# Column tiles of 32 instead of 64 for the packed up tail in a fused attention and gated feed-forward kernel

## The chip, the cores and the metric

One core of a Trainium2 chip runs the whole kernel. The metric is the device time of one execution in microseconds (us). The kernel before takes 195.24 us, the median of three runs (195.07 to 195.54). The profiler's span is some 1.7 us shorter, 193.5 us for the profiled execution, and the granted clock of TensorE in it was 1.000.

## The reference

One residual block over 2048 tokens of width 512, all in bfloat16. A layer norm feeds two branches, and both are added to the input.

```python
def reference(...):                                    # cut
    xn = layernorm(A_x)
    # A: 32 heads of 16; each token attends to itself and 7 earlier ones, 2 apart
    qkv = xn @ A_wqkv
    logits[h, s, w] = q[h, s] . k[h, s - 2 w] * 16 ** -0.5      # masked for s < 2 w
    o = softmax(logits) @ v[h, s - 2 w]
    a = o @ A_wo
    # B: gated feed-forward, inner width 1376 = 10 * 128 + 96
    b = (gelu(xn @ B_w_gate) * (xn @ B_w_up)) @ B_w_down
    return A_x + a + b
```

## The kernel before

The kernel is a list of tasks, one per group of instructions of one engine, with the buffers that they read and write. A list scheduler orders them by priority and puts in the semaphores; the table `SHIFT` moves groups of tasks up and down in priority. The 2048 tokens go through in four blocks of 512.

The inner width of 1376 leaves a tail of 96 columns after ten full tiles of 128. The gate tail, with 32 of the up columns, is one ordinary group of four 512-column matmuls (L1409). The other 64 up columns are packed: the 512 tokens are cut into two halves of 256, and each half goes into its own 64 columns of the array, so that two matmuls run side by side. They share one task with the sums over head elements that make the attention logits, which use four 32-column tiles side by side. I call this task the logit group.

```python
def mk_r(...):                     # the logit group of one block, on TensorE (L1208, L1215)
    def f(e):
        for kt in range(4):
            for c in range(2):     # two tiles of 64 columns, 256 tokens each
                ins = e.matmul(PS[64 * c:64 * c + 64, 512 * itu.slot:512 * itu.slot + 256],
                               lhsT=Wt[:, kt, 128:192],
                               rhs=xnT[:, itx.slot, kt, 256 * c:256 * c + 256],
                               start=(kt == 0), stop=(kt == 3), tile_position=(0, 64 * c))
        for (g, prs) in grp:       # 4 x 2 rounds of four tiles of 32 columns, 512 elements each
            for wq in range(2):
                for sj in range(4):
                    ins = e.matmul(PS[32 * sj:32 * sj + 32, ...], lhsT=E8[:, 24 - 8 * g:56 - 8 * g],
                                   rhs=UNI[:, prs[wq].slot, :, sj * 128:(sj + 1) * 128],
                                   start=(g == 0), stop=(g == 3), tile_position=(0, 32 * sj))
        return ins
```

The weighted sum over values (L1342) is also made of rounds of four 32-column tiles, and in blocks 1 and 2 it directly precedes the logit group. The other lines named below are the query, key and value projections (L1077 in block 0's start, L1131 elsewhere), the feed-forward matmuls (L1374), and the final accumulation over the attention output and the down projection (L1449, L1453).

Of the kernel before, what the change touches and what calls it, by code (L numbers as in the profile page):

```python
# [145 lines left out]
class Graph:  # L146
# [478 lines left out]


SHIFT = {
    "acc0": 223, "acc1": 3251, "er1": 857, "er2": 1563, "er3": -682, "ffn0": 185, "ffn1": -481, "ffn3": 9,
    "fin1": -264, "fin2": 595, "fin3": -2, "h0": -264, "h1": 24, "h2": 384, "h3": 81, "ldb0": 811,
    "ldb2": 200, "ldb3": -487, "ln1": 29, "ln2": 123, "ln3": -821, "prod0": 131, "prod1": -198, "pv0": 31,  # L630
    "pv1": -32, "pv2": 2520, "pv3": -241, "pvr0": 93, "pvr1": 556, "pvr2": 1268, "qkv1": 36, "qkv3": 44,
    "sm0": 114, "sm1": 276, "sm2": 146,
}
SCHED = dict(PE_SLACK=1.6, DMA_BPUS=250e3,
             TOL=dict(pe=0.3, act=-0.3, dve=0.3, pool=-0.3, sp=0.0))
# [24 lines left out]
def d_dve(n, rate=1.04):  # L660
    return 0.07 + n * rate * 1e-3
# [6 lines left out]
def bass_parallel_sum__sliding_local_dilated__glu_gated_geglu__prompt_kernel(nc, A_x, A_wqkv, A_wo, B_x, B_w_gate, B_w_up, B_w_down, out, dbg=None, cfg=None):  # L668
# [41 lines left out]
    with contextlib.ExitStack() as es:  # L710
        block = es.enter_context(nc.Block())

        def sb(name, shape, dt):
            return es.enter_context(nc.sbuf_tensor(name, shape, dt))
# [4 lines left out]
        Wt = sb("Wt", [128, 4, 192], BF)  # L719
        Wd = sb("Wd", [128, NJ, 512], BF)  # L720
        Wo = sb("Wo", [128, 4, 512], BF)
        xnT = sb("xnT", [128, NXT, 4, 512], BF)
# [32 lines left out]
        PS = es.enter_context(nc.psum_tensor("PS", [128, 4096], F32))  # L755
# [302 lines left out]
        for b in range(NB):  # L1058
# [119 lines left out]
            for g in range(4):  # L1178
                prs = []
                for wq in range(2):  # L1180
                    it_pr = pr_items[g][wq]
                    prs.append(it_pr)

                    def mk_p(wq=wq, g=g, it=it_pr, itq=it_qt, itk=KTI[b]):
                        return lambda e: e.tensor_tensor(  # L1185
                            out=UNI[:, it.slot, :, :],
                            in0=bass.AP(QT, (itq.slot * 4 + g) * 512, [[NQT * 4 * 512, 128], [0, 4], [1, 512]]),
                            in1=bass.AP(KT, (itk.slot * 4 + g) * 528 + 4 - 2 * wq, [[2 * 4 * 528, 128], [4, 4], [1, 512]]),
                            op=ALU.mult)
                    rdk = ([(KTI[0], ("t", t)) for t in range(4)] if b == 0 else [(KTI[b], g)]) + [(KTI[b], "pad")]  # L1190
                    rdq = [(it_qt, ("t", t)) for t in range(4)] if b == 0 else [(it_qt, (g, 0))]
                    t_of["pr%d_%d_%d" % (b, wq, g)] = G.task("dve", "pr%d_%d_%d" % (b, wq, g), d_dve(2048, 0.52), mk_p(),
                           rd=rdq + rdk, wr=[(it_pr, "d")] + ([(q, "a") for gg in range(g, g + ER_MERGE) for q in pr_items[gg]
                                                      if q is not it_pr] if g % ER_MERGE == 0 and wq == 0 else []),
                           prio=base + 20)

                er_grp.append((g, prs))
                if len(er_grp) < ER_MERGE:
                    continue

                it_u10 = Item("u%d_10" % b, P_ps, "ffn")

                def mk_r(grp=list(er_grp), lg=it_lg, itu=it_u10, itx=XTI[b]):
                    def f(e):
                        ins = None
                        for kt in range(4):
                            for c in range(2):
                                ins = e.matmul(PS[64 * c:64 * c + 64, 512 * itu.slot:512 * itu.slot + 256],  # L1208
                                               lhsT=Wt[:, kt, 128:192],
                                               rhs=xnT[:, itx.slot, kt, 256 * c:256 * c + 256],  # L1210
                                               start=(kt == 0), stop=(kt == 3), tile_position=(0, 64 * c))
                        for (g, prs) in grp:
                            for wq in range(2):
                                for sj in range(4):
                                    ins = e.matmul(  # L1215
                                        PS[32 * sj:32 * sj + 32, 512 * (lg.slot + wq):512 * (lg.slot + wq) + 512],
                                        lhsT=E8[:, 24 - 8 * g:56 - 8 * g],
# [3 lines that stand above are left out]
                    return f  # L1221
                G.task("pe", "er%d_%d" % (b, g), 0.4315 * (ER_MERGE + 1), mk_r(),
                       rd=[q for g_ in er_grp for q in g_[1]] + [I_E8, XTI[b], (I_wt, 2)],
                       wr=[it_lg, it_u10], prio=base + 5, mode="c", util=0.8)
                er_grp = []
# [316 lines left out]
```

## Time and profile before

| | kernel before |
|---|---|
| time, median of 3 | 195.24 us |
| span of the profiled execution | 193.5 us |
| busy: TensorE, VectorE, ScalarE | 97%, 79%, 54% |
| chain that ended last: TensorE | 93% |
| TensorE's waits for other engines after 6.3 us | none |
| last accumulation group begins; last addition begins | 190.22 us; 191.10 us |

The page's chain is followed back from the last instruction, and the views of waits name what an engine waited for. The prediction below shows the lines that carry this. The end of the kernel before, from the timeline (start us, us, engine, line, form; the bracket gives the idle time before it and what ended it):

```profile
190.22 0.78 PE L1453 MATMUL PS<-Wd,HT 128*128 128x128 bf16 x11
191.10 0.29 DVE L1473 TENSOR_TENSOR OB<-PS,XR 128x128 bf16<-128x128 f32 x1 [0.55 <-PE PS L1453]
```

The last addition begins 0.88 us after the last group of matmuls begins, and what it waits for is TensorE.

### The profile page before, as it was taken

Reading aid. Unit: us, or ns where it says so; the run is one execution under the profiler, and the core shown is the slowest. Engines: PE = TensorE matmul, PEld = TensorE weight load, DVE = VectorE, ACT = ScalarE, POOL = GpSimd, SP = SyncE. Lnnn points to the kernel's source line nnn. Section 1 sums busy time; section 2 is a strip of 40 time slices with the busy share of each in tenths; the row PEclk is TensorE's granted clock in tenths of the full one; section 3 lists DMA queues with packets and bytes.
Section 4 is the critical chain, followed back from the end, with each engine's and each line's share of the span. In section 5 each row is a group of like instructions: output and inputs, shape, how many; then the busy total and the mean of one; then the engine's idle time right before and its main releaser. Section 6 shows DMA issues by size and latency. Waiting matters only on the chain.

```text
span 193.5 us, 3221 instructions
## 1 busy us (share of the span) xinstructions
PE 187.4 (97%) x1207; PEld 91.6 (47%) x1224; DVE 153.2 (79%) x241; ACT 104.0 (54%) x171; POOL 16.2 (8%) x31
## 2 busy tenths in 40 slices
PE   6899999999999999999999999999999999999994
PEld 2794444444444444444444444444444444444484
DVE  5898999999998988995895699988997089931132
ACT  3587583996676665501667777328266640048000
POOL 6013001014711000000200000000000000000000
DMA  5999999898375006953511587420250298130121
GB/s 134 354 396 305 327 168 178 216 277 186 71 181 106 2 3 160 234 156 105 181 36 50 140 216 157 130 77 0 68 128 21 62 243 189 54 112 0 44 79 41
DMA packets 34800, 27.03 MB, mean 140 GB/s; under 512 B 11265, under 2 KB 33249, under 8 KB 34785
## 3 DMA queue, kind: packets, MB, share of 16 engines
q1 hardware_dynamic: 34784, 26.83, 54.6%
q8 instruction: 9, 0.15, 0.3%
q14 instruction: 7, 0.05, 0.1%
HBM read 19.99 MB, written 5.26 MB: 131 GB/s over the span
## 4 chain that ended last, share of the span: by engine, by line
PE 93%; ACT 2%; DVE 2%; DMA 1%; issue 1%; DVEq 0%
PE PS L1374 34%; PE PS L1453 20%; PE PS L1131 18%; PE PS L1449 7%; PE PS L1077 4%; PE PS L1342 4%; PE PS L1215 4%; PE PS L1409 1%; PE PS L1208 1%; DMA XIN<-in_A_x_dram 1%; ACT OT L1354 1%; DVE st L937 1%; PE PS L1019 0%; ACT UU L1391 0%; DVE XIN L976 0%
## 5 line engine op out<-in xcount | busy, mean ns | idle before, releaser
L1453 PE MATMUL PS<-Wd,HT 128*128 128x512 bf16 (+2 forms) x207 | 41.2, 345 | 0.1
L1374 PE MATMUL PS<-xnT,Wu 128*128 128x512 bf16 x157 | 39.9, 379 | 0.3 <-issue 0.2
L1374 PE MATMUL PS<-xnT,Wg 128*128 128x512 bf16 x154 | 39.3, 379 | 0.7 <-issue 0.5
L1185 DVE TENSOR_TENSOR UNI<-QT,KT 128x2048 bf16<-128x2048 bf16 x32 | 37.2, 1221 | 2.3 <-PE PS L1342 1.5
L1384 ACT ACTIVATE GG<-PS 128x512 bf16<-128x512 f32 x40 | 23.8, 601 | 26.5 <-PE PS L1374 23.1
L1131 PE MATMUL PS<-xnT,Wqkv 128*128 128x512 bf16 x156 | 34.8, 379 | 0.3 <-issue 0.2
L1391 ACT ACTIVATE UU<-PS 128x512 bf16<-128x512 f32 x40 | 24.0, 599 | 15.6 <-PE PS L1374 15.6
L1396 DVE TENSOR_TENSOR HT<-GG,UU 128x512 bf16<-128x512 bf16 x40 | 16.2, 418 | 17.3 <-ACT UU L1391 17.1
L1453 PEld LDWEIGHTS PS<-Wd,HT 128*128 128x128 bf16 x209 | 19.6, 98 | 18.6
L1374 PEld LDWEIGHTS PS<-xnT,Wg 128*128 128x128 bf16 x160 | 15.4, 98 | 19.4 <-issue 0.8
L1374 PEld LDWEIGHTS PS<-xnT,Wu 128*128 128x128 bf16 x160 | 15.5, 98 | 19.3 <-issue 0.8
L1131 PEld LDWEIGHTS PS<-xnT,Wqkv 128*128 128x128 bf16 x160 | 15.5, 98 | 18.8 <-ACT OT L1354 0.4
L1473 DVE TENSOR_TENSOR OB<-PS,XR 128x512 bf16<-128x512 f32 (+2 forms) x19 | 11.4, 602 | 11.8 <-PE PS L1453 11.6
L1322 DVE TENSOR_TENSOR UNI<-BS,PT 128x2048 bf16<-128x2048 bf16 x16 | 19.5, 1219 | 0.6 <-DMA PT<-pt_scratch 0.5
L1322 DVE TENSOR_TENSOR BS<-BS,PT 128x2048 bf16<-128x2048 bf16 x16 | 19.6, 1222 | 0.3
L1449 PE MATMUL PS<-Wo,OT 128*128 128x512 bf16 (+2 forms) x75 | 16.7, 345 | 0.1
L1148 ACT ACTIVATE KT<-PS 128x512 bf16<-128x512 f32 x12 | 7.3, 606 | 14.3 <-PE PS L1131 14.3
L1155 ACT ACTIVATE VT<-PS 128x512 bf16<-128x512 f32 x16 | 9.6, 597 | 4.4 <-PE PS L1131 4.4
L937 DVE BATCH_NORM_STATS2 st<-XIN 128x6 f32<-128x512 bf16 x16 | 10.7, 685 | 1.0 <-DMA XIN<-in_A_x_dram 1.0
L1171 POOL COPY KT<-KT 128x64 bf16<-128x64 bf16 x3 | 7.6, 2518 | 40.0 <-ACT KT L1148 38.6
L1354 ACT ACTIVATE OT<-PS 128x512 bf16<-128x512 f32 x16 | 8.3, 602 | 4.3 <-PE PS L1342 4.3
L1449 PEld LDWEIGHTS PS<-Wo,OT 128*128 128x128 bf16 x76 | 7.2, 98 | 7.0
(66 smaller groups left out, 150.3 us busy)
## 6 DMA issues: line engine op xcount, KB each, us to landing
BS<-vt_scratch SPq DMA_DIRECT2D x64, 128.5 KB, 3.5
vt_scratch<-VT SPq DMA_DIRECT2D x16, 128.0 KB
XR<-in_A_x_dram SPq DMA_DIRECT2D x16, 128.0 KB, 2.2
out_dram<-OB SPq DMA_DIRECT2D x14, 128.0 KB, 2.1
Wqkv<-in_A_wqkv_dram SPq DMA_DIRECT2D x3, 512.0 KB
XIN<-in_A_x_dram SPq DMA_DIRECT2D x6, 256.0 KB, 5.8
Wg<-in_B_w_gate_dram SPq DMA_DIRECT2D x1, 1280.0 KB
Wu<-in_B_w_up_dram SPq DMA_DIRECT2D x1, 1280.0 KB
```

Source lines behind the costliest of these rows:

```text
L937: return lambda e: e.bn_stats(out=st[:, t, :], in_=XIN[:, it.slot, t2, :])
L1131: ins = e.matmul(PS[:, 512 * it.slot:512 * it.slot + HWD], lhsT=lhsT, rhs=xnT[:, itx.slot, kt, c0:c0 + HWD], start=(kt == 0), stop=(kt == 3))
L1185: return lambda e: e.tensor_tensor(out=UNI[:, it.slot, :, :], in0=bass.AP(QT, (itq.slot * 4 + g) * 512, [[NQT * 4 * 512, 128], [0, 4], [1, ...
L1322: return lambda e: e.tensor_tensor(out=dst(), in0=bass.AP(BS, it.slot * 4 * 514 + o, [[NBS * 4 * 514, 128], [514, 4], [128, 4], [1, 128]]) ...
L1354: return lambda e: e.activation(out=OT[:, ito.slot, dq, :], in_=PS[:, 512 * it.slot:512 * it.slot + 512], func=ACTF.Identity)
L1374: ins = e.matmul(PS[0:M, 512 * it.slot:512 * it.slot + 512], lhsT=Wx[:, kt, j * 128:j * 128 + M], rhs=xnT[:, itx.slot, kt, :], start=(kt = ...
L1384: return lambda e: e.activation(out=GG[0:M, ito.slot, :], in_=PS[0:M, 512 * it.slot:512 * it.slot + 512], func=ACTF.Gelu_apprx_tanh)
L1391: return lambda e: e.activation(out=UU[0:M, ito.slot, :], in_=PS[0:M, 512 * it.slot:512 * it.slot + 512], func=ACTF.Identity)
L1396: return lambda e: e.tensor_tensor(out=HT[0:M, ito.slot, j, :], in0=GG[0:M, ig.slot, :], in1=UU[0:M, iu.slot, :], op=ALU.mult)
L1449: ins = e.matmul(PS[:, 512 * it.slot:512 * it.slot + CW], lhsT=OT[:, ito.slot, dq, ti * 128:(ti + 1) * 128], rhs=Wo[:, dq, c0:c1], start=( ...
L1453: ins = e.matmul(PS[:, 512 * it.slot:512 * it.slot + CW], lhsT=HT[:, ith.slot, j, ti * 128:(ti + 1) * 128], rhs=Wd[:, j, c0:c1], start=Fal ...
L1473: return lambda e: e.tensor_tensor(out=OB[:, ito.slot, 0:CW], in0=PS[:, 512 * it.slot:512 * it.slot + CW], in1=XR[:, itx.slot, c0:c1], op= ...
```

## The change

The 64 packed up columns are cut into two pieces of 32, so that four matmuls of 32 columns run side by side instead of two of 64, in the shape of the sums around them. The intent is that TensorE does not change its tile width inside the group. The table of priority shifts was searched again along with it, which reorders the tasks of all engines.

```diff
 SHIFT = {
-    "acc0": 223, "acc1": 3251, "er1": 857, "er2": 1563, "er3": -682, ...            # cut
+    "acc1": 4275, "er1": 814, "er2": 3235, "er3": -369, "fin0": 704, ...            # cut
 }
@@
                         for kt in range(4):
-                            for c in range(2):
-                                ins = e.matmul(PS[64 * c:64 * c + 64, 512 * itu.slot:512 * itu.slot + 256],
-                                               lhsT=Wt[:, kt, 128:192],
-                                               rhs=xnT[:, itx.slot, kt, 256 * c:256 * c + 256],
-                                               start=(kt == 0), stop=(kt == 3), tile_position=(0, 64 * c))
+                            for c in range(4):
+                                ins = e.matmul(PS[32 * c:32 * c + 32, 512 * itu.slot:512 * itu.slot + 256],
+                                               lhsT=Wt[:, kt, 128 + 32 * (c % 2):160 + 32 * (c % 2)],
+                                               rhs=xnT[:, itx.slot, kt, 256 * (c // 2):256 * (c // 2) + 256],
+                                               start=(kt == 0), stop=(kt == 3), tile_position=(0, 32 * c))
```

## The prediction

> **What bounds the kernel now.** I read the page first (busy shares, slices, the chain that ended last), then the waits of TensorE, then the timeline around the sums that the diff touches.
>
> ```profile
> PE 187.4 (97%) x1207; PEld 91.6 (47%) x1224; DVE 153.2 (79%) x241; ACT 104.0 (54%) x171; POOL 16.2 (8%) x31
> PE   6899999999999999999999999999999999999994
> PE 93%; ACT 2%; DVE 2%; DMA 1%; issue 1%; DVEq 0%
> ```
>
> TensorE is busy in every slice and carries 93% of the chain. A busy TensorE need not be at its limit, so the waits decide:
>
> ```profile
> PE PS L863 <- DVE wsrc L812: 1.5, 1, 1.5
> PE PS L1077 <- DVE rstd L969: 0.7, 1, 0.7
> PE PS L1374 <- issue: 0.6, 4, 0.2
> PE PS L1131 <- issue: 0.2, 1, 0.2
> ```
>
> That is the whole list: TensorE's columns are line waited for, total us, times, longest. The first two lie in the first 6.3 us. After that the matmuls wait for no other engine; what is left are five small "issue" gaps, which I take apart below. The head (0 to 6.26 us, load and layer norm) and the end (last matmul group ends at 191.01, then one addition and the store, to 193.5) are not touched by the new tile shape. In between lie 184.7 us in which every us of TensorE is a us of the kernel.
>
> The streaming rate comes from the chain in order of time (start us, us, what):
>
> ```profile
> 177.94 0.86 PE PS L1449 x4
> ...
> 184.41 0.44 PE PS L1449 x4
> ```
>
> Four matmuls of 512 columns take 0.86 us, 0.216 each; four of 256 columns take 0.44, 0.109 each.
>
> Now the touched group, in block 0 and in block 1 (timeline of TensorE: start us, us until the modelled end, line, form, count):
>
> ```profile
> 28.52 0.59 PE L1374 MATMUL PS<-xnT,Wu 128*128 128x512 bf16 x2
> 29.05 0.63 PE L1208 MATMUL PS<-xnT,Wt 128*64 128x256 bf16 x8
> 29.61 1.91 PE L1215 MATMUL PS<-UNI,E 128*32 128x512 bf16 x32
> 31.68 0.59 PE L1374 MATMUL PS<-xnT,Wg 128*128 128x512 bf16 x2 [0.16 <-issue]
> ```
>
> ```profile
> 72.57 0.39 PE L1342 MATMUL PS<-UNI,E 128*32 128x512 bf16 x4
> 72.79 0.39 PE L1342 MATMUL PS<-BS,E 128*32 128x512 bf16 x4
> 73.11 0.63 PE L1208 MATMUL PS<-xnT,Wt 128*64 128x256 bf16 x8
> 73.67 1.91 PE L1215 MATMUL PS<-UNI,E 128*32 128x512 bf16 x32
> ```
>
> Starts are trustworthy, modelled ends are not, so I subtract starts. 28.52 to 29.05 is 0.53 us for two matmuls that stream in 0.43: about 0.09 to 0.10 us is lost where the array passes from 128-column to 64-column tiles. L1208 is 8 matmuls in 4 rounds of 2 side by side, 4 x 0.109 = 0.44 us, but 0.56 us pass until L1215 begins: 0.12 us lost passing from 64 to 32. In block 1 the group follows the 32-wide sums of L1342 directly: 72.79 to 73.11 is 0.32 us for one round of 0.216, 0.10 lost going 32 to 64, then 0.12 lost going back to 32 (73.11 to 73.67).
>
> The way out of L1215 in block 0 looks worse than it is. 29.61 to 31.68 is 2.07 us for 8 rounds of 0.216 (1.73), a rest of 0.34. But the page's groups show matmul records missing:
>
> ```profile
> L1374 PE MATMUL PS<-xnT,Wu 128*128 128x512 bf16 x157 | 39.9, 379 | 0.3 <-issue 0.2
> L1374 PE MATMUL PS<-xnT,Wg 128*128 128x512 bf16 x154 | 39.3, 379 | 0.7 <-issue 0.5
> L1374 PEld LDWEIGHTS PS<-xnT,Wg 128*128 128x128 bf16 x160 | 15.4, 98 | 19.4 <-issue 0.8
> ```
>
> 160 weight loads stand against 154 matmuls, and one unrecorded 512-column matmul is 0.216 us, so the true loss is about 0.12 us, and the 0.16 us "issue" is mostly an artefact. I choose not to count it as recoverable; the change keeps this way out.
>
> **What the Trainium skill says.** "TensorEngine Tiling (Array Packing)", section Tiling Modes, Key Properties: "Changing tiling mode (not just tile) drains the TensorE". The trace agrees and gives the size: 0.09 to 0.12 us at each change of width. "TensorE: Matmul & The Clock Gate", section Back-to-back issue gap, gives N / 2.4 + 2.5 ns; at 256 and 512 columns that is 109 and 216 ns, as measured. The same page, section "Wait — 56ns, not 53.3ns?", says that starts never come closer than about 25 ns on average. The new shape needs four matmuls in 109 ns, 27 ns each, close to that floor; the trace of before has nothing denser than 54 ns per matmul sustained (8 rounds of 4 in 216 ns each, or pairs in 109), so no run here yet shows whether the floor bites.
>
> **The change, part by part.**
>
> *Tile shape.* Work in the array is the same: 8 matmuls of 64x256 in 4 rounds of two become 16 of 32x256 in 4 rounds of four, 4 x 0.109 = 0.44 us either way, over four blocks 32 more matmuls and 32 more weight loads. The weight loads are not the limit: the 64-wide ones took 110 ns and the 32-wide ones of L1215 97 ns (median of each line's records), below a round's 109.
>
> What goes away are changes of width, all on the path that sets the end:
> - Blocks 0 and 3, preceded by full-width matmuls (28.52 and 125.83): 128 to 64 to 32 becomes 128 to 32. The entry stays at its 0.09 (L1342 is entered from full width for the same price), one loss of 0.12 goes. 2 x 0.12 = 0.24 us.
> - Blocks 1 and 2, preceded by L1342 (72.79 and 108.21): 32 to 64 to 32 becomes no change at all. 2 x (0.10 + 0.12) = 0.44 us.
>
> Sum 0.68 us, 0.35% of the time. This assumes the new order still puts L1342 directly ahead of the group in blocks 1 and 2. It should: the scheduler gives a 32-wide task absolute priority while the array is in that mode, and the new shifts (er1 814, er2 3235) still hold these groups back. If block 3's group also met an L1342, another change in and one out, some 0.2 us, would go; with er3 early and pv2 late in both tables I don't expect it.
>
> *New priority shifts.* They add and remove no instruction, they reorder. Since TensorE has no wait to lose after 6.3 us, reordering can't gain in the middle; it can at most keep zero waits, or add some. The head's waits are in a fixed chain of tasks. The scheduler keeps 1.6 us of slack between another engine's result and its use on TensorE (PE_SLACK), in both versions, so I book only 0.1 us for new waits.
>
> Sum: 195.24 - 0.68 + 0.1 = 194.66, which I round to 194.6.
>
> **Rivals.**
> 1. *Issue binds the denser group.* 16 loads and 16 matmuls in 0.44 us. If each matmul and its load cost the 54 ns seen today, the group takes 0.86 instead of 0.44 us, 4 x 0.43 = 1.7 us more, and the net is about +1.0, 196.3 us. For it: nothing denser is in the trace. Against it: within a round of L1215 four starts lie within some 10 ns, so queued instructions leave fast, and slower 512-column matmuls run ahead of the group, which lets a queue fill. I give it one in ten, and half of it at most.
> 2. *The new order makes TensorE wait.* VectorE is at 79%, and about 90% up to 125 us, and the groups wait on its products; a product that comes 1 us late costs 1 us. For it: the table changes nearly wholesale (acc1 by 1000, er2 by 1700). Against it: the slack, and that today's order has no wait at all with the same scheduler. It would give 195 to 196.
> 3. *Nothing is gained*, if the drain is per group, not per change of width: 195.2. Against it: among L1215's eight rounds, and where L1342 goes from one of its four groups to the next, starts stay 0.216 apart.
> 4. *More than I count*: 0.2 us from another junction, 0.2 us in the head: 194.2.
>
> **Range and chances.** Rivals 1 and 2 lie above, so the range is longer on that side: 194.1 to 195.5. Faster by over 2% means below 191.3; TensorE's streaming alone forbids it, since all changes of width together (four groups and two lone L1342 groups, at 0.1 to 0.12 each) are about 2 us: chance 0.01. Slower by over 2% is above 199.1 and needs 4 us of new waits: 0.02.
>
> **What would show it.** L1208 should have 64 matmuls of 128*32 with starts 0.109 us apart by rounds of four, and L1215 should begin about 0.44 us after L1208 (today 0.56). In blocks 1 and 2, L1208 should begin 0.22 us after the last round of L1342 (today 0.32). TensorE's waits on other engines after 6.3 us should stay absent. I am wrong if L1208's rounds are wider than 0.12 us (rival 1), if TensorE shows waits on ACT or DVE (rival 2), or if the gap at the junctions stays (rival 3).

## More of the kernel before

Every accumulated piece is added to the input by VectorE into an output buffer `OB` and stored. There are three such buffers, and the last two row tiles of 128 tokens (14 and 15) are cut into two and three pieces:

```python
NOB = cfg.get("NOB", 3)
TAIL_SPLIT = {14: [(0, 256), (256, 512)], 15: [(0, 256), (256, 384), (384, 512)]}
...
def mk_fin(...):                   # L1473, VectorE
    return lambda e: e.tensor_tensor(out=OB[:, ito.slot, 0:CW], in0=PS[...], in1=XR[...], op=ALU.add)
def mk_so(...):                    # L1480, store
    return lambda e: e.dma_start(out2[128 * t:128 * t + 128, c0:c1], OB[:, it.slot, 0:CW])
```

The last addition uses the buffer of the piece three places earlier, the second half of row tile 14, so it cannot begin until that store has landed.

## The result, and the profile after

The changed kernel takes 195.04 us, the median of six runs (194.65 to 195.36); six runs of the kernel before beside it gave 195.23 us. The ratio is 0.9988 with a 95% interval of 0.9973 to 1.0004. The time lies in the predicted range and, as forecast, within 2% of the kernel before, but the gain of the medians is 0.19 us where the predicted 194.6 means 0.64, and the sum of the junctions alone was 0.68.

In the changed kernel all lines stand one lower: L1208 is L1207, L1453 is L1452, and so on. From its page, busy times, TensorE's slices and the chain:

```profile
PE 187.4 (97%) x1239; PEld 92.6 (48%) x1256; DVE 153.0 (79%) x241; ACT 104.3 (54%) x171; POOL 15.6 (8%) x31
PE   6999999999999999999999999999999999999993
PE 95%; DMA 2%; issue 1%; DVE 1%; ACT 0%; DVEq 0%
```

TensorE has 32 more matmuls and 32 more weight loads and is as busy as before. A DMA has entered the chain with 2%. The waits of TensorE (line waited for, total us, times, longest):

```profile
PE PS L862 <- DVE wsrc L811: 1.5, 1, 1.5
PE PS L1373 <- issue: 0.6, 4, 0.2
PE PS L1373 <- ACT OT L1353: 0.3, 2, 0.2
```

The two 0.2 us waits on ScalarE stand where the array leaves the 32-wide tiles, in the place of such "issue" gaps; a matmul record is missing there, as the prediction worked out, so I take them for no waits (the split kernel below bears that out). The junctions in block 1, from TensorE's timeline:

```profile
74.71 0.39 PE L1341 MATMUL PS<-BS,E 128*32 128x512 bf16 x4
74.93 0.61 PE L1207 MATMUL PS<-xnT,Wt 128*32 128x256 bf16 x16
75.37 1.90 PE L1214 MATMUL PS<-UNI,E 128*32 128x512 bf16 x32
```

From 74.71 to 74.93 is 0.22 us, one round of 0.216 and no loss (0.32 before). L1207 to L1214 is 0.44 us, four rounds of 0.109 and no loss (0.56 before). So the junctions do what was predicted. To see where the gain went I cut the profiled execution into three parts: up to the last group of query and key projections of block 0, which has 48 matmuls and the same place in both orders; from there to the last accumulation group; and from there to the last addition.

| profiled execution | group of 48 begins | last accumulation begins | difference | last addition begins | difference |
|---|---|---|---|---|---|
| before | 11.60 | 190.22 | 178.62 | 191.10 | 0.88 |
| after | 11.92 | 189.83 | 177.91 | 191.20 | 1.37 |

The middle is 0.71 us shorter. The head is 0.32 us longer and the end 0.49 us longer, so this execution shows nothing of the gain: -0.71 + 0.32 + 0.49 = +0.10 us, as its span of 193.6 instead of 193.5 says. It was also the slowest of the six, 195.36 us. The end, from the timeline and then in the chain in order of time:

```profile
189.83 0.78 PE L1452 MATMUL PS<-Wd,HT 128*128 128x128 bf16 x11
191.20 0.29 DVE L1472 TENSOR_TENSOR OB<-PS,XR 128x128 bf16<-128x128 f32 x1 [1.03 <-DMA out_dram<-OB]
```

```profile
187.40 0.43 DVE OB L1472
187.84 0.02 issue
187.85 3.33 DMA out_dram<-OB
191.18 0.02 issue
191.20 0.29 DVE OB L1472
```

The last addition no longer waits for TensorE. It waits for the store of the second half of row tile 14, issued at 187.85, which takes 3.33 us and holds the third output buffer. The same store of the kernel before was issued at 188.24 and landed 1.53 us later, by the landing records of its trace (each store leaves sixteen; I count to the last). What else used the DMA engines then, in the view of DMA from 187 to 193.5 us (queue, kind: packets, MB, share; issues: count, KB each, us to landing), first before, then after:

```profile
q14 instruction: 1, 0.01, 0.5%
```

```profile
q8 instruction: 1, 0.02, 1.5%
q14 instruction: 1, 0.01, 0.3%
out_dram<-OB SPq DMA_DIRECT2D x2, 64.0 KB, 3.3
```

Queue q8 carries 16 KB blocks of instructions. The kernel before has nine such loads in its whole span and none after 174 us; the changed kernel has ten, and the tenth begins at 188.59 us, lasts 1.54 us, and overlaps the store. Of the sixteen landings of that store, as many as the core has DMA engines, fifteen come by 189.4 us and one at 191.18. This gave the theory that the experiments test: the 64 more TensorE instructions push the stream over the edge of one more block, and that load holds one DMA engine while the store is on it.

The head is a matter of TensorE's first microseconds. The first group of projections, from the timelines before and after:

```profile
6.26 0.61 PE L1077 MATMUL PS<-xnT,Wqkv 128*128 128x128 bf16 x8 [0.65 <-DVE rstd L969]
```

```profile
6.29 0.90 PE L1076 MATMUL PS<-xnT,Wqkv 128*128 128x128 bf16 x8
```

The same eight matmuls take 0.90 instead of 0.61 us. In the trace of after, matmuls of 128 columns are still 107 ns apart until 6.9 us, where those of before are 56 ns apart from 4.95 us on. TensorE's order is the same in both kernels up to this point. Over all twelve profiled executions the group of 48 begins between 11.56 and 12.08 us (table below). The Trainium skill, page "TensorE: Matmul & The Clock Gate", section Part 1: The HAM clock gate, says that the array starts at half rate and that the point where it rises depends on a window that does not start with the kernel. The spacings agree with two rates; what sets the point was not tested here.

### The profile page after: what moved, and what is told of

Read it like the earlier page. It is cut to its first block, busy times and chain, and to the rows that moved or that the text cites. A ratio compares the mean times of both kernels' runs of the same rounds, so it can differ in the third digit from the quotient of the medians.

```text
span 193.6 us, 3277 instructions
## 1 busy us (share of the span) xinstructions
PE 187.4 (97%) x1239; PEld 92.6 (48%) x1256; DVE 153.0 (79%) x241; ACT 104.3 (54%) x171; POOL 15.6 (8%) x31
## 4 chain that ended last, share of the span: by engine, by line
PE 95%; DMA 2%; issue 1%; DVE 1%; ACT 0%; DVEq 0%
PE PS L1373 35%; PE PS L1452 18%; PE PS L1130 18%; PE PS L1448 7%; PE PS L1076 4%; PE PS L1341 4%; PE PS L1214 4%; PE PS L862 2%; DMA out_dram<-OB 2%; PE PS L1408 2%; PE PS L1207 1%; PE PS L1018 1%; DVE OB L1472 0%; ACT xnT L1038 0%; DVE wsrc L811 0%
## 5 line engine op out<-in xcount | busy, mean ns | idle before, releaser
L1452 PE MATMUL PS<-Wd,HT 128*128 128x512 bf16 (+2 forms) x207 | 41.1, 345 | 0.1
L1130 PE MATMUL PS<-xnT,Wqkv 128*128 128x512 bf16 x156 | 35.3, 379 | 0.2
L1452 PEld LDWEIGHTS PS<-Wd,HT 128*128 128x128 bf16 x209 | 19.6, 98 | 18.6
L936 DVE BATCH_NORM_STATS2 st<-XIN 128x6 f32<-128x512 bf16 x16 | 10.8, 685 | 0.9 <-DMA XIN<-in_A_x_dram 0.9
L1140 ACT ACTIVATE QT<-PS 128x512 bf16<-128x512 f32 x12 | 7.2, 597 | 3.1 <-PE PS L1130 3.1
```

Source lines behind the costliest of these rows:

```text
L936: return lambda e: e.bn_stats(out=st[:, t, :], in_=XIN[:, it.slot, t2, :])
L1130: ins = e.matmul(PS[:, 512 * it.slot:512 * it.slot + HWD], lhsT=lhsT, rhs=xnT[:, itx.slot, kt, c0:c0 + HWD], start=(kt == 0), stop=(kt == 3))
L1452: ins = e.matmul(PS[:, 512 * it.slot:512 * it.slot + CW], lhsT=HT[:, ith.slot, j, ti * 128:(ti + 1) * 128], rhs=Wd[:, j, c0:c1], start=Fal ...
```

## The experiments

Theory A: the junctions save 0.71 us whatever else happens, and the rest is chance in the head and in the store. Theory B: the new order of tasks costs what is missing. Theory C: the shorter middle brings the tail onto the store systematically. Theory D, formed after the first four runs: the instruction count causes the late store. All ten runs gave correct results. Each was timed in five rounds beside the kernel before, in three sets on three chips; its median was 195.35 us in each set.

The expectations speak of a stretch from the first V matmul. Its record is missing in some traces, which moves that start by 0.216 us, so I give the stretch of the table above instead: 178.62 us for before is their 175.73, and 177.91 is their 175.02.

| kernel | time, us | ratio | group of 48 begins | stretch | to the last addition | 16 KB load near the end: start, us | store of tile 14's second half, us |
|---|---|---|---|---|---|---|---|
| before | 195.24 | 1 | 11.60 | 178.62 | 0.88 | none | 1.53 |
| after | 195.04 | 0.9988 | 11.92 | 177.91 | 1.37 | 188.59, 1.54 | 3.33 |
| after again | 194.85 | 0.9975 | 11.58 | 177.91 | 1.26 | 188.24, 1.38 | 3.20 |
| tile shape only | 194.80 | 0.9969 | 12.08 | 177.91 | 0.89 | 188.40, 0.95 | 2.38 |
| order only | 195.16 | 0.9991 | 11.56 | 178.63 | 0.88 | none | 1.53 |
| 64-wide, split | 196.30 | 1.0050 | 11.83 | 179.57 | 0.88 | none | 1.53 |
| 32-wide, split | 194.75 | 0.9969 | 11.93 | 177.91 | 0.88 | 188.22, 0.89 | 2.42 |
| before, 64 instructions more | 195.54 | 1.0007 | 12.03 | 178.70 | 0.89 | 189.18, 0.95 | 2.42 |
| after, 96 instructions more | 194.76 | 0.9972 | 11.79 | 178.03 | 0.88 | 181.81, 0.95 | 1.53 |
| after, four buffers | 194.64 | 0.9959 | 11.64 | 177.91 | 0.88 | 188.27, 1.13 | 2.93 |
| before, four buffers | 195.34 | 0.9997 | 11.57 | 178.62 | 0.88 | none | 1.53 |
| tile shape only, four buffers | 194.64 | 0.9961 | 11.79 | 177.91 | 0.88 | 188.16, 1.15 | 2.64 |

Times are medians; the columns right of the ratio are read from the one profiled execution of each kernel. The last column is from the issue of the store to the last of its sixteen landings.

### The changed kernel once more

No edit.

> The changed kernel once more, to see how often its late points come back. Theory A (chance: the clock of TensorE rises later in some runs, +0.3 us, and the store that frees the last output buffer lands late in some runs, +0.5 us): the median falls somewhere between 194.5 and 195.2, spread about 0.7 us, and in the profile at least one of the two delays is different from the 0.3 and 0.5 us of the first profile. Theory B (the delays belong to the new order): 195.0 again, and the profile shows the last addition waiting about 1.0 us for a store again. TensorE's last group begins near 189.8 us in both.

The median was 194.85 us (194.59 to 195.40, six runs), ratio 0.9975 (0.9961 to 0.9989). The head was short this time, 11.58 us, but the store was late again, 3.20 us, and the last addition waited for it:

```profile
190.75 0.29 DVE L1472 TENSOR_TENSOR OB<-PS,XR 128x128 bf16<-128x128 f32 x1 [0.91 <-DMA out_dram<-OB]
```

So the head is chance and the late store is not only chance. Neither theory as I put it was right.

### Tile shape only, and order only

The two halves of the change, each alone: the new matmuls with the old `SHIFT`, and the old matmuls with the new `SHIFT`.

```diff
 tile shape only: SHIFT as before, matmuls as after
 order only:      SHIFT as after,  matmuls as before
```

> Tile shape of the change, priority shifts of before. The four junctions save 0.71 us whatever the order. Theory A: same median as the changed kernel within 0.2 us, 194.5 to 195.0. Theory B (the new order costs some 0.5 us and eats the gain): 194.5, clearly below the changed kernel.

> Priority shifts of the change, 64-wide tiles of before. Theory A (order is worth nothing): 195.2, as before, ratio 1.000 within 0.001. Theory B (the order costs): 195.7, ratio 1.0025. In both the trace shows losses of 0.10 and 0.12 us around L1207 again.

The tile shape alone gives 194.80 us, ratio 0.9969 (0.9957 to 0.9981); the order alone 195.16 us, ratio 0.9991 (0.9979 to 1.0003), not told from 1. The stretch is 177.91 and 178.63 us, so all 0.71 us come from the tile shape and none from the order. Theory B, which wanted 194.5 and 195.7, falls. The shape-only kernel has the tenth load and the late store too (2.38 us), without a wait.

### Four output buffers in the changed kernel

```diff
-    NOB = cfg.get("NOB", 3)
+    NOB = cfg.get("NOB", 4)
```

The order of instructions stays the same on every engine except for one load that moves past a store on the DMA queue in the middle of the kernel, and a few semaphore instructions.

> The changed kernel with four output buffers instead of three, so that the last addition no longer needs the store of the third piece back. Theory A and a third theory C (the store wait is there in most runs, because the tail now reaches it earlier): the wait of the addition on a store is gone. C: median 194.4 to 194.6, 0.3 to 0.5 below the changed kernel beside it. A: 0.1 to 0.2 below. If the store wait was only in the one profiled run: no difference.

It took 194.64 us (194.40 to 194.65), ratio 0.9959 (0.9947 to 0.9971), 0.21 us below the changed kernel in the same rounds, between what A and C wanted. The store is late as ever and the last addition does not care:

```profile
out_dram<-OB SPq DMA_DIRECT2D x2, 64.0 KB, 2.9
```

```profile
190.43 0.29 DVE L1472 TENSOR_TENSOR OB<-PS,XR 128x128 bf16<-128x128 f32 x1 [0.55 <-PE PS L1452]
```

The medians show the whole 0.71 us of the junctions, 195.35 - 194.64. By the ratio the gain is 0.80 us (0.57 to 1.04), so the agreement to a hundredth is luck. This run also does not change the buffer alone: the 8 KB load on queue q14 came 2.0 us before the last accumulation group where it came 0.4 us before it in the changed kernel, and the store landed at 190.50 us, so that even with three buffers the addition would have waited less than 0.1 us in this execution.

### The sums split, 64-wide and 32-wide

To test that the loss belongs to each change of width, the packed tail comes in two halves, one ahead of and one between the 32-wide sums. The instruction count does not change.

```diff
-                        for kt in range(4):
-                            for c in range(2):
-                                ...
-                        for (g, prs) in grp:
-                            ...
+                        for part in range(2):
+                            for kt in (2 * part, 2 * part + 1):
+                                for c in range(2):          # range(4) in the 32-wide version
+                                    ...
+                            for (g, prs) in grp[2 * part:2 * part + 2]:
+                                ...
```

> Kernel before, but in each block the 64-wide sums come in two halves, one ahead of and one between the 32-wide sums: two more changes of width per block, no instruction more. Junction theory (each change of width costs 0.10 to 0.13 us): 4 x 0.23 = 0.94 us more, TensorE from the first V matmul to its last group 176.67 us instead of 175.73, median about 196.2 to 196.3, ratio 1.0048. Rival (the cost belongs to the group as a whole or to its slow first round): less than 0.3 us more.

> The same split with 32-wide tiles (order of before, so the shape-only kernel with the split). Junction theory: the split costs nothing, TensorE's stretch stays 175.02 us, median 194.8 as the shape-only kernel. Rival (splitting itself costs, by more groups): as much more as in the 64-wide one, 195.7.

64-wide: 196.30 us, ratio 1.0050 (1.0038 to 1.0062), and the stretch is 179.57 us, 0.95 us more for eight more changes of width, 0.12 us each. 32-wide: 194.75 us, stretch 177.91, no cost at all. The 64-wide block 1 in TensorE's timeline:

```profile
73.26 0.39 PE L1343 MATMUL PS<-BS,E 128*32 128x512 bf16 x4
73.58 0.41 PE L1209 MATMUL PS<-xnT,Wt 128*64 128x256 bf16 x4
73.92 1.05 PE L1216 MATMUL PS<-UNI,E 128*32 128x512 bf16 x16
74.89 0.41 PE L1209 MATMUL PS<-xnT,Wt 128*64 128x256 bf16 x4
75.23 1.05 PE L1216 MATMUL PS<-UNI,E 128*32 128x512 bf16 x16
76.21 0.61 PE L1131 MATMUL PS<-xnT,Wqkv 128*128 128x512 bf16 x2
```

Two rounds of the tail stream in 0.22 us but take 0.34 each time (73.58 to 73.92, 74.89 to 75.23), and four rounds of sums, 0.86, take 0.97 (73.92 to 74.89). No matmul record is missing from this trace, and here the way out is 75.23 to 76.21, 0.98 us, of which four rounds are 0.86: the loss is 0.12 us. This trace shows no "issue" gap either, which confirms that the 0.16 us gaps of the other traces were missing records.

### 64 instructions more in the kernel before

The gate tail's four 512-column matmuls of each block are cut into twelve narrower ones: 32 more matmuls and 32 more weight loads, without any change of width.

```diff
-                    for kt in range(4):
-                        ins = e.matmul(PS[:, 512 * it.slot:512 * it.slot + 512], lhsT=Wt[:, kt, 0:128],
-                                       rhs=xnT[:, itx.slot, kt, :], start=(kt == 0), stop=(kt == 3))
+                    for c0, c1 in ((0, 192), (192, 352), (352, 512)):
+                        for kt in range(4):
+                            ins = e.matmul(PS[:, 512 * it.slot + c0:512 * it.slot + c1], lhsT=Wt[:, kt, 0:128],
+                                           rhs=xnT[:, itx.slot, kt, c0:c1], start=(kt == 0), stop=(kt == 3))
```

> Kernel before, 64-wide, with the gate tail's four 512-column matmuls in each block cut into twelve of 160 or 192 columns: 64 more TensorE instructions, as many as the change adds, no change of width. Theory D (these instructions cause a tenth 16 KB instruction load near 188.5 us, which holds one DMA engine and delays the store of the second half of row tile 14): ten instead of nine loads on queue q8, the last near 188.5 us, that store lands 2.4 to 3.4 us after issue instead of 1.5, and the last addition waits on a store for up to 0.5 us in runs where it is long. Streaming costs 0.08 us more (32 x 2.5 ns). Median 195.4 to 195.7. Rival (late stores come from the 32-wide tiles or by chance): nine loads, store in 1.5 us, 195.4.

The tenth load appeared, at 189.18 us, and the store took 2.4 us instead of 1.5 (DMA from 187 to 192 us):

```profile
q8 instruction: 1, 0.02, 1.2%
...
out_dram<-OB SPq DMA_DIRECT2D x3, 64.0 KB, 2.4
```

The 2.4 in this line is the median of three stores; the store in question took 2.42 us by its landing records. So the load and the late store follow the instruction count and not the 32-wide tiles. In this execution the last addition did not wait: the store's delay was 0.9 us. The stretch grew by 0.08 us, as worked out. The time, 195.54 us with a ratio of 1.0007 (0.9993 to 1.0021), does not separate the theories.

### 96 instructions more in the changed kernel

```diff
+                    for c0, c1 in ((0, 128), (128, 256), (256, 384), (384, 512)):     # otherwise as above
```

> The changed kernel with 96 more TensorE instructions (gate tail cut in four), which brings the tenth instruction load some 5 us forward, to about 183 us, away from the last stores. Theory D: the last addition no longer waits on a store, the store lands in about 1.5 us; 0.12 us more streaming, so 194.65 to 194.85, spread as small as with four output buffers. Rival (the late store belongs to the tail itself): the wait of 0.9 to 1.0 us stays, median 194.95 to 195.1.

The tenth load moved to 181.81 us, nothing of queue q8 is left after 187 us, the store lands in 1.53 us and the last addition waits for TensorE alone:

```profile
out_dram<-OB SPq DMA_DIRECT2D x2, 64.0 KB, 1.5
```

```profile
190.70 0.29 DVE L1473 TENSOR_TENSOR OB<-PS,XR 128x128 bf16<-128x128 f32 x1 [0.55 <-PE PS L1453]
```

With 96 instructions more and a stretch 0.12 us longer it took 194.76 us, 0.09 less than the changed kernel (in another set of rounds, so within what two sets differ by). Theory C falls with this trace: the middle is as short but for the 0.12 us, and the wait is gone.

### Four buffers without the tile shape, and without the new order

The edit of four buffers, in the kernel before and in the shape-only kernel.

> Kernel before with four output buffers. It has nine instruction loads and its last addition waited for TensorE, not for a store. Theory D: nothing to gain, ratio 1.000 within 0.001. Rival (a fourth buffer is worth 0.2 us or more by itself, whatever the instruction count): 195.1 or less, ratio 0.999.

> 32-wide tiles, priority shifts of before, four output buffers: the candidate to beat both. Junctions give 0.71 us, the late store costs nothing: 194.6 (194.5 to 194.7), ratio 0.9963, equal to the changed kernel with four buffers within 0.1 us. Rival (the old order gains something of its own): 194.4 or less.

In the kernel before the fourth buffer is worth nothing that can be measured (195.34 us, ratio 0.9997, interval 0.9985 to 1.0009): nine loads, no late store, nothing to cure. The old order with the new tiles and four buffers takes 194.64 us (194.33 to 194.96), the same as the new order with four buffers. Both have the tenth load, the late store and no wait. These two have the lowest medians found, but their intervals overlap that of the tile shape alone (194.80 us), which showed no wait in its trace with three buffers.

## Why the prediction was right or wrong

**The junctions** were right in mechanism and nearly in size: 0.68 us predicted, 0.71 measured in every trace with the new tiles (in the one with 96 instructions more, once their 0.12 us are taken off). The 0.03 us lie in blocks 1 and 2. The first round after a change of width is slow: 133 ns instead of 109 in the 64-wide tiles, 120 in the 32-wide ones, and 226 instead of 216 in the first round of L1215. In blocks 1 and 2 L1214 no longer has a slow first round, 0.01 us in each, which I did not count (in blocks 0 and 3 the slow first round of L1207 takes that back); the rest is rounding. The rounding of 194.66 to 194.6 was a slip: it is 194.7.

**L1342 would still stand directly ahead of the group in blocks 1 and 2:** right, and block 3 stayed alone as expected.

**Rival 1, issue:** it does not bind. Four matmuls with their weight loads go through in 109 ns, 27 ns each, for a run of 16. On the rate itself, the section Back-to-back issue gap that the prediction cites gives its formula for a lone matmul, and some 131 ns for each 512-column matmul in a stream with weight loads; these traces, with a load for each, show 216, so the measurement decides.

**Rival 2, new waits of TensorE, and the order:** right that there are none. The order alone is worth nothing that can be measured.

**Rival 3, loss per group:** refuted by the split kernels, 0.95 us against 0.

**Rival 4, more than counted:** 0.03 us in the middle; the head moved by chance.

**The range** held for a reason that it did not foresee. It was drawn up to 195.5 for rivals 1 and 2, neither of which came; the first median, 195.04, lies above 194.6 through the store and perhaps the head. That is luck. The 0.1 us booked for new waits of TensorE did not come either.

**What failed** is a sentence at the start of the prediction: "The head (0 to 6.26 us, load and layer norm) and the end (last matmul group ends at 191.01, then one addition and the store, to 193.5) are not touched by the new tile shape." I counted the 64 new instructions and asked only whether TensorE could issue them fast enough. I did not ask what loading them does. They cause a tenth 16 KB load, in the last 5 us, which makes one of the sixteen landings late of a store that the last addition depends on. In all seven traces with this load after 188 us, the late landing comes 1.05 to 1.18 us after the load's end; which DMA engine carried which, the traces don't say. The numbers of the wait fit: the store of before was issued at 188.24 and the last addition began at 191.10, so a landing time of up to about 2.85 us is free. The landing of 3.33 us should cost 0.48, and it cost 0.49 (1.37 - 0.88); that of 3.20 should cost 0.35 and cost 0.38; those of 2.38 and 2.42 cost nothing. With four buffers 2.93 costs nothing either.

The Trainium skill has pieces that point there. Its page "Runtime: NRT & Kernel Launch", section Instruction fetch mechanics, says that instructions come in blocks of 16 KiB, 256 instructions, over a DMA queue of the sequencer's own, and calls the cost "mostly hidden". The trace agrees on the block size, and TensorE itself never waited for one. Its page "DMA: Bandwidth & Descriptors", section Queues, rings and completion order, says that each DMA engine takes turns between its queues a whole packet at a time; one late landing of sixteen during a 16 KB load is what that would look like.

**What stays open.** The load itself took 1.54 and 1.38 us in the two profiled executions of the changed kernel, and 0.89 to 1.15 in the five other traces in which it came after 188 us; only in the former did the last addition wait. In those two traces an 8 KB load on queue q14 falls into the 16 KB one, at 189.0 to 189.5 us; in the five others it comes ahead of it. Its place follows the order: it begins 0.3 to 0.5 us before the last accumulation group in all four traces of the new order with three buffers, and 2.4 to 3.2 us before it in all seven of the old order. That this overlap is what made the 16 KB load long, and so the addition wait, is argued, not shown: it rests on two traces, earlier 16 KB loads took up to 3.4 us, and the shape-only and the changed kernel differ by 0.05 us in time, too little to tell. How often the wait comes in unprofiled executions isn't known either. The changed kernel's second set scattered from 194.59 to 195.40 us, and with four buffers from 194.40 to 194.65; but the shape-only kernel with four buffers scattered from 194.33 to 194.96, so the spread of five or six runs proves little. The head's 0.5 us between executions, and so part of the first measured median, was seen and not explained by a test.

## What to carry to other kernels

Where TensorE bounds a kernel, count its changes of column tile width: each cost about 0.12 us here, so sums in the shape of their neighbours are free while an odd one costs two changes. When a change adds instructions, look also at where the loads of instruction blocks then fall: one in the last microseconds can delay a store that frees a buffer. Before you trust a gain in the middle, check that the end of the kernel still waits for the engine that got faster, and give the last pieces enough buffers that none has to be returned.

## What the Trainium skill lacked or had wrong

- "TensorEngine Tiling (Array Packing)", Key Properties, says that a change of tiling mode drains TensorE and gives no cost. The runs show 0.12 us for each change, the slow first round included (0.95 us for eight), the same order of size among 128, 64 and 32 columns, and nothing between groups of one width.
- "TensorE: Matmul & The Clock Gate", section LDWEIGHTS (loading the stationary operand), gives load times in proportion to the number of columns, P / 1.2 ns, 53 and 27 ns for 64 and 32 columns. The records show 110 and 97 ns (98 for 128 columns), in a stream that still took a new round every 109 ns; whether a record holds waiting besides the loading was not tested. The page's floor of about 25 ns between starts (section "Wait — 56ns, not 53.3ns?") holds here as an average only: four side by side start 3 to 4 ns apart, and a round of four takes 109 ns, 27 each, with a weight load for each matmul.
- "Runtime: NRT & Kernel Launch", section Instruction fetch mechanics, calls the cost of crossing a block boundary mostly hidden. It was hidden from TensorE, but the 16 KB load took 0.89 to 1.54 us near the end of these kernels and one of the sixteen landings of a 64 KB store came 0.9 to 1.8 us late. No page that I read warns of this.
- No page that I read says that matmul records can be missing and leave apparent "issue" gaps: 17 of 1224 in the trace of before, often 10.8 us apart, nearly all of them matmuls of 0.216 us, and none in the trace of the 64-wide split.
